# A gated linear-attention stage feeding a bilinear layer: larger bf16 product groups, paired state updates, a gate table in two parts

## The chip, the core and the metric

One NeuronCore of a Trainium2 chip. The metric is the device time of one execution in microseconds, the median over several runs; a profiled execution, taken apart from those runs, gives the span and all the rows below. TensorE is written PE, its weight loads PEld, VectorE DVE, ScalarE ACT, GpSimd POOL, and the queue of the sync engine, which issues all transfers here, SP.

## The reference

Inputs: q, k, v and an output gate of shape (4 batches, 8 heads, 768 steps, 40), two gates per step and head, and three weight matrices in float64 (two of 320x1536, one of 1536x320).

```python
for t in range(S):
    m_new = np.maximum(f_gate[:, :, t] + m, i_gate[:, :, t])
    f_stab = np.exp(f_gate[:, :, t] + m - m_new)
    i_stab = np.exp(i_gate[:, :, t] - m_new)
    m = m_new
    C = f_stab[..., None, None] * C + i_stab[..., None, None] * np.einsum('bhd,bhe->bhde', vt, kt)
    n = f_stab[:, :, None] * n + i_stab[:, :, None] * kt
    h_tilde = np.einsum('bhde,bhe->bhd', C, qt)
    denom = np.maximum(np.abs(np.einsum('bhd,bhd->bh', n, qt)[:, :, None]), 1.0)
    y[:, :, t] = sigmoid(o_gate[:, :, t]) * h_tilde / denom
x = y.transpose(0, 2, 1, 3).reshape(3072, 320)
out = ((x @ w_a) * (x @ w_b)) @ w_out
```

## The kernel before

**Chunks.** The 768 steps are cut into 6 time chunks of 128 rows for each of 4 batches: 24 chunks, numbered n = 4c + b. Within a chunk the recurrence becomes products: `pS` (keys times queries), multiplied by a decay matrix `E` (tile `gbc`), then `pV` (that times the values), plus `pI` (queries times the state before the chunk). `pU` is the chunk's addition to the state `cst`; `pT` and `pE` are transposes and the decay matrix of early chunks; `pX` transposes the finished rows into `xh` and `xl`. Chunks 0 to 5 use plain float32 products (`begin_a`, `begin_b`, `begin_i`, `begin_c`); from chunk 6 on every float32 operand is split into three bf16 parts and a product becomes several bf16 ones (`stage_a`, `stage_b`, `stage_i`, `stage_c`). A bf16 `pS` has 8 products for half the heads, a `pI` 16, a `pV` 48.

**The layer.** The 24 chunks are gathered in nine blocks of 2 or 3 chunks (256 or 384 rows). For each of 12 slices of the hidden width, `up` does 2 x 8 products `pu` (fp32r, from `xh`, `xl` and weight parts), DVE multiplies the two results into `g`, `gh` and `gl` are split off, and `down` does 3 products `pd` per chunk. Products `pu` and `pd` of 384, 256 and 320 columns are most of PE's work.

**Weights.** They come as float64 in 32 stages (`fetch`, `raw`). Each is turned into two fp32r parts: `high` on ACT, `low` on DVE or ACT, `join` on DVE, `lead_part` a copy on either, `low_part` a subtraction on DVE (tiles `cw` and `w`). `weights()` does stages 5 to 31 while block 0 runs; the last one, stage 31, is needed by the last `down` of block 0.

**Gates.** `first_gates` makes what chunks 0 to 3 need for their decay matrix. `later_gates` runs scans over steps 128 to 767 (32 rows of 640 on DVE, tiles `qks`), writes a table to DRAM (`g_dram`, read back by `load_g` as `gbc`), and transposes it (`ptg`) into `gtab`, which holds columns for weights of values (`w_col`), for decay (`a_col`), and so on. In `rest()` it runs before anything of chunk 2.

**The order.** Nothing is issued as written. A recorder (`Plan.add`) turns each call into a node; PE calls that follow each other and write the same tile (or carry `plan.pair`) form one node of at most 8. `Plan.run` is a list scheduler with a cost table, ranks and queues per engine; `settle` runs it 40 times with disturbed ranks and keeps the order with the least planned end; `emit` writes that order down. Operations of `copier` may go to ACT or DVE, those of `adder` to DVE or POOL. Where PE would idle early on, the plan inserts filler products into a tile `warm`. All instructions issued by `emit` carry line 522 (fillers 515), so the profile is read by tiles.

**State.** `stage_u` (line 1066) works chunk by chunk: 8 float32 products `pU` into half a bank, ACT copies or DVE updates `cst[b]`, and from chunk 2 on the state is split into bf16 parts (`cb`, `cr`), written to DRAM (`put_state`, `c_dram`) and read back (`get_state`, `cx`). `load(n + 2)` in `aside` fetches q, k and v two chunks ahead into three rotating tiles (`qk`, `va`).

Of the kernel before, what the change touches and what calls it, by code (L numbers as in the profile page):

```python
# [21 lines left out]
TURNS = 40  # L22
TRIALS = 4
# [7 lines left out]
SPELL = 3.4133  # L31

# [75 lines left out]
class Node:  # L108
    __slots__ = ("i", "eng", "alts", "calls", "by", "prev", "next", "table", "acc", "wide", "use", "pair", "least")

    def __init__(self, i, alts):
        self.i, self.alts, self.eng = i, alts, alts[0]
        self.calls, self.prev, self.next, self.acc = [], {}, [], []
        self.by = {e: [0.0, 0.0, 0.0, False] for e in alts}
        self.table, self.wide, self.use = None, True, 0.0


class Plan:
# [9 lines left out]
    def __init__(self, nc):  # L128
        self.nc, self.nodes, self.filler, self.bank = nc, [], None, None
        self.pair, self.least = False, 0.0  # L130
# [8 lines left out]
    def add(self, engines, op, args, kw):  # L139
# [13 lines left out]
        if not (  # L153
            alts[0] == "PE" and node is not None and node.eng == "PE" and len(node.calls) < 8
# [26 lines left out]
    def cost(self, node, by, eng, op, out, refs, args, kw):  # L181
# [5 lines left out]
        if eng == "PE":  # L187
            if op == "transpose":
                occ = 0.109
            else:  # L190
# [3 lines left out]
                elif "float32r" in f32[0]:  # L194
                    occ = cols / 2400 + 0.0135
# [7 lines left out]
            by[1] = 0.17  # L203
            plain = size[1] == 4 and op == "matmul" and "float32r" not in f32[0]
# [34 lines left out]
    def link(self):  # L239
        last, rings = {}, {}  # L240
        for node in self.nodes:
            for key, box, write in node.acc:
# [16 lines left out]
                mine.append((node, box, write))  # L259
        for ring in rings.values():  # L260
# [23 lines left out]
    def run(self, rank, forward=True, fixed=None, odds=None):  # L284
# [18 lines left out]
        order, count, filling = [], 0, False  # L303
# [21 lines left out]
        def choose(e, t):  # L325
# [6 lines left out]
            while ready[e] and found is None:  # L332
# [16 lines left out]
                else:  # L349
                    found = i  # L350
            for z in back:
                heapq.heappush(ready[e], z)
# [5 lines left out]
        while count < len(nodes):  # L358
# [56 lines left out]
            if e == "PE" and forward:  # L415
# [5 lines left out]
                z = free[e] + 0.2  # L421
                while filling and fixed is None:
                    w = int((z + phase) / SPELL)
                    z += 0.107 if used.get(w - 1, 0.0) >= 0.375 * SPELL * 2400 else 0.214
                    if z > t:
                        break
                    used[w] = used.get(w, 0.0) + 256
                    order.append(None)
                w = int((t + phase) / SPELL)
# [45 lines left out]
    def settle(self):  # L475
# [6 lines left out]
            (rng.uniform(0.98, 1.07, n), 1.0 + 0.025 * j, 0.1 * j, SPELL * j / TRIALS)  # L482
# [70 lines left out]
def kernel(  # L553
# [64 lines left out]
    cst = [wpool.tile([P, HH, DV], F32, name=f"cst{b}") for b in range(B)]  # L618
# [85 lines left out]
    def squash(c, b, nb):  # L704
        x = osig[c][:, b:b + nb, 0:DM]
        nc.scalar.activation(x, x, AF.Sigmoid)

# [43 lines left out]

    def later_gates():
# [8 lines left out]
        nc.scalar.copy(G[:, 0], gb3[0][:, 0])  # L761
        nc.scalar.copy(tab[BH:2 * BH, 0], gb3[0][:, 1])
        for c in range(1, NC):
# [6 lines left out]
        nc.sync.dma_start(g_dram.rearrange("c g t -> g c t"), G)  # L770
# [10 lines left out]
            tab[2 * BH:], tab[BH:2 * BH], G[:, :, P - 1:P].broadcast_to([BH, NC, P]), op=ALU.add  # L781
        )
        yield
        for half in range(2):
            pt = ps_dn.tile([P, 512], F32, tag="pd2", name="ptg")
            n3 = NC // 2
            for c in range(n3):
                nc.tensor.transpose(
                    pt[:, c * 3 * BH:(c + 1) * 3 * BH], tab[:, half * n3 + c, :],
                    ident[0:3 * BH, 0:3 * BH],  # L790
                )
            n0, n1 = (BH, n3 * 3 * BH) if half == 0 else (0, (n3 * 3 - 1) * BH)
# [4 lines left out]
        x = gtab[:, BH:].rearrange("p (c g) -> p c g", g=3 * BH)[:, :, 0:2 * BH]  # L797
# [9 lines left out]
    def g_col(c, b, x):  # L807
        return gtab[:, (3 * c + x) * BH + b * H:][:, 0:H]
# [7 lines left out]
    def a_col(c, b):  # L816
        return g_col(c - 1, b, 2)
# [165 lines left out]
    def stage_v(n):  # L983
        s = st[n]
        x = nat(n)[1]
        vr = apool.tile([P, H, DV], F32, tag="vr", name=f"vr{n}")
        vl = apool.tile([P, H, DV], BF16, tag="vl", name=f"vl{n}")
# [49 lines left out]
    def stage_c(n):  # L1037
# [4 lines left out]
        if c < NC - 1:  # L1042
            vw = apool.tile([P, H, DV], F32, tag="vw", name=f"vw{n}", bufs=1)
# [22 lines left out]
    def stage_u(n):  # L1066
        c, b = chunks[n]
        if c == NC - 1:
            return
        s = st[n]  # L1070
# [4 lines left out]
        pu = pU[:, 0:HH * DV].rearrange("p (h d) -> p h d", h=HH)  # L1075
        for h in range(H):
            r, _, x = half(h)
            nc.tensor.matmul(
                pu[r:r + 64, x], nat(n)[0][:, 1, h, :], s["vw"][:, h], start=True, stop=True
            )  # L1080
        t = cst[b]
        if c == 0:
            nc.scalar.copy(t, pu)
        else:
            nc.vector.tensor_tensor(
                t, t, dec[:, c - 1, b * HH:(b + 1) * HH].unsqueeze(2).broadcast_to([P, HH, DV]),
# [4 lines left out]
        if n + B < NF32:  # L1091
            return
        cb = apool.tile([P, 3, HH, DV], BF16, tag="cb", name=f"cb{n}", bufs=1)
        cr = apool.tile([P, H * DV], F32, tag="tmp", name=f"cr{n}")[:, 0:HH * DV]
        cr = cr.rearrange("t (h d) -> t h d", h=HH)
        nc.scalar.copy(cb[:, 2], t)
        nc.gpsimd.tensor_tensor(cr, t, cb[:, 2], op=ALU.subtract)
        yield
        if n < 8:
            nc.scalar.copy(cb[:, 1], cr)  # L1100
        else:
            nc.vector.tensor_copy(cb[:, 1], cr)
        nc.gpsimd.tensor_tensor(cb[:, 0], cr, cb[:, 1], op=ALU.subtract)
        states[n] = cb
        yield
# [46 lines left out]
    def stage_d(n):  # L1152
        s = st[n] if n < NS else st.pop(n)
# [25 lines left out]
    def aside(o, n):  # L1179
        if o == "L" and n + 2 < NCH and n + 2 > NS + 1:  # L1180
            load(n + 2)
        if o == "P":
            put_state(n - 1)
        if o == "G" and NE < n + 2 < NCH:
            load_g(n + 2)
        if o == "C":
            get_state(n - 1)
# [40 lines left out]
    def attention():  # L1228
        for n in range(NS, NCH):
# [369 lines left out]
```

## Time and profile before

| | before |
|---|---|
| median of 3 runs | 534.64 us (534.57 to 535.79) |
| profiled execution: own time | 534.12 us |
| profiled execution: span | 532.3 us |
| PE busy | 523.2 us (98%) |
| DVE busy | 411.4 us (77%) |
| ACT busy | 236.3 us (44%) |
| POOL busy | 147.9 us (28%) |

In a timeline row the first number is the start in microseconds from the span's beginning, the second the length, then engine, line, operation, tiles (output, arrow, inputs), shapes, and x with the number of instructions merged; a bracket tells idle time ahead and what ended it. PE's matmuls are pipelined: their records overlap, so what one costs is read from start to start, not from its length. A plain float32 product appears as two records.

### The profile page before, as it was taken

What the parts mean: (1) busy time and instruction counts of PE and PEld (TensorE: products, weight loads), DVE (VectorE), ACT (ScalarE), POOL (GpSimd) and SP (SyncE); (2) the same over time, 40 slices, a digit from 0 to 9 for tenths busy, and PEclk for the clock granted to TensorE, in tenths of its full rate; (3) what the DMA queues carried; (4) which work ended last, traced back from release to release, by engine and by line L of the source; (5) the groups of instructions that cost most, each with busy time, mean ns of one, the idle gap of its engine ahead of it and who ended that gap; (6) DMA issues with size and microseconds to landing.
All of it is one profiled execution on the core that took longest, in us unless ns stands there. A gap on an engine that the chain in (4) does not pass through costs nothing.

```text
span 532.3 us, 12505 instructions
## 1 busy us (share of the span) xinstructions
PE 523.2 (98%) x4862; PEld 497.1 (93%) x4862; DVE 411.4 (77%) x919; ACT 236.3 (44%) x568; POOL 147.9 (28%) x194
## 2 busy tenths in 40 slices
PE   8889999999999999999999999999999999999997
PEld 6679999999999999999999999999999999999997
DVE  5999999799979859888599776888489848843332
ACT  5759997543456142346243344543215515212111
POOL 2015134414326505534223423526050301000000
PEclk9899999999999999999999999999999999999999
DMA  9998866978696864886755766765537427000001
GB/s 172 305 245 182 238 167 135 137 148 165 117 188 129 148 146 104 155 158 104 169 105 97 158 119 157 155 99 114 130 73 140 93 41 156 2 1 25 2 1 37
DMA packets 198679, 66.77 MB, mean 125 GB/s; under 512 B 184252, under 2 KB 191900, under 8 KB 198620
## 3 DMA queue, kind: packets, MB, share of 16 engines
q1 hardware_dynamic: 198620, 65.98, 59.6%
q8 instruction: 38, 0.62, 0.5%
q14 instruction: 21, 0.17, 0.1%
HBM read 41.11 MB, written 5.97 MB: 88 GB/s over the span
## 4 chain that ended last, share of the span: by engine, by line
PE 81%; DVE 7%; issue 3%; DMA 2%; ACT 2%; SPq 1%; POOL 0%; ACTq 0%; DVEq 0%; POOLq 0%
PE pu L522 46%; PE pd L522 22%; PE pV L522 4%; PE pS L522 3%; PE pU L522 2%; DVE qks L522 2%; DVE w L522 2%; PE pI L522 2%; SPq L522 1%; PE pX L522 1%; DMA qk<-in_k_dram 1%; DVE cw L522 1%; DMA gbc<-g_dram 1%; DMA c_dram<-cb 1%; DVE osig L522 1%
## 5 line engine op out<-in xcount | busy, mean ns | idle before, releaser
L522 PE MATMUL pu<-xh,w 128*128 128x384 f32 (+1 forms) x1080 | 277.2, 325 | 0.1
L522 PE MATMUL pu<-xl,w 128*128 128x384 f32 (+1 forms) x648 | 203.9, 323 | 0.9 <-DVE xl L522 0.9
L522 PEld LDWEIGHTS pu<-xh,w 128*128 128x128 f32 x1080 | 190.0, 189 | 1.7 <-ACT xh L522 0.6
L522 PE MATMUL pd<-w,gh 128*128 128x320 f32 x576 | 135.1, 315 | 0.3 <-ACT gh L522 0.2
L522 PEld LDWEIGHTS pu<-xl,w 128*128 128x128 f32 x648 | 121.1, 189 | 1.4 <-DVE xl L522 1.2
L522 PEld LDWEIGHTS pd<-w,gh 128*128 128x128 f32 x576 | 97.0, 188 | 1.0 <-ACT gh L522 0.7
L522 DVE TENSOR_TENSOR g<-pu,g 128x384 f32<-128x384 f32 (+1 forms) x108 | 54.6, 506 | 53.4 <-PE pu L522 50.2
L522 ACT COPY g<-pu 128x384 f32<-128x384 f32 (+1 forms) x99 | 43.7, 442 | 113.8 <-PE pu L522 112.6
L522 PE MATMUL pd<-w,gl 128*128 128x320 f32 x288 | 86.6, 310 | 0.1
L522 ACT ACTIVATE gbc<-gbc,gtab 128x128 f32<-128x128 f32 x160 | 52.7, 394 | 3.3 <-POOL gbc L522 3.3
L522 PEld LDWEIGHTS pd<-w,gl 128*128 128x128 f32 x288 | 53.4, 188 | 0.3 <-DVE gl L522 0.3
L522 POOL TENSOR_TENSOR gl<-g,gh 128x384 fp32r<-128x384 f32 (+1 forms) x24 | 26.4, 1102 | 81.4 <-ACT gh L522 46.0
L522 DVE TENSOR_TENSOR gl<-g,gh 128x384 fp32r<-128x384 f32 (+1 forms) x84 | 46.4, 553 | 2.1 <-DVE gh L522 0.5
L522 ACT CAST gh<-g 128x384 fp32r<-128x384 f32 (+1 forms) x44 | 20.5, 465 | 39.9 <-DVE g L522 39.8
L522 DVE TENSOR_TENSOR gbc<-pS,gbc 128x512 f32<-128x512 f32 x48 | 32.6, 681 | 4.7 <-ACT gbc L522 3.7
L522 POOL TENSOR_TENSOR vr<-va 128x336 f32<-128x336 f32 x18 | 14.0, 775 | 79.0 <-PE pV L522 71.1
L522 PE MATMUL pV<-va,gbc 128*128 128x42 bf16 (+1 forms) x240 | 34.5, 221 | 0.0
L522 POOL TENSOR_TENSOR vw<-va,gtab 128x336 f32<-128x336 f32 x20 | 16.2, 808 | 64.9 <-PE pU L522 58.1
L522 PEld LDWEIGHTS <-T 120*128 120x128 bf16 x576 | 25.4, 97 | 7.6 <-issue 5.1
L522 DVE TENSOR_TENSOR gbc<-gbc,pb 128x512 f32<-128x512 f32 x36 | 29.4, 817 | 0.4 <-ACT pb L522 0.3
L522 DVE TENSOR_TENSOR pb<-gbc 128x512 bf16<-128x512 f32 x36 | 29.0, 806 | 0.3
L522 POOL TENSOR_SCALAR_AFFINE_SELECT gbc<-gbc 128x1024 f32<-128x1024 f32 x20 | 25.0, 1248 | 11.7 <-DMA gbc<-g_dram 11.7
(109 smaller groups left out, 768.7 us busy)
## 6 DMA issues: line engine op xcount, KB each, us to landing
gbc<-g_dram SPq DMA_DIRECT2D x20, 512.0 KB
qk<-in_q_dram SPq DMA_DIRECT2D x24, 160.0 KB
qk<-in_k_dram SPq DMA_DIRECT2D x24, 160.0 KB
va<-in_v_dram SPq DMA_DIRECT2D x24, 160.0 KB
osig<-in_o_gate_dram SPq DMA_DIRECT2D x24, 160.0 KB
raw<-in_moe_w_out_dram SPq DMA_DIRECT2D x12, 320.0 KB
out_dram<-o SPq DMA_DIRECT2D x24, 160.0 KB
raw<-in_moe_w_a_dram SPq DMA_DIRECT2D x8, 384.0 KB
```

The costliest lines, as they stand in the source:

```text
L522: f(*[real(x) for x in args], **{k: real(x) for k, x in kw.items()})
```

## The change

The planner gets other rules and the recorder larger groups; the state update takes two chunks at a time; the gate table for time chunk 0 is made apart from the rest.

- **Groups.** A PE node may hold 24 calls if its operand is bf16, 16 if paired, else 8 as before. In the scheduler a PE node whose first weight load is longer than the product ahead of it can hide is put back if another ready node, within `BAND` of its rank, is of the short kind; so short products follow each other. The cost table prices that load and the switch between full and half array. Filler rules are new (`GAP`, `FULL`, `LEAST`, `FORCED`), the disturbances in `settle` are other ones, and it makes 100 turns.
- **Pairs.** `stage_u` does nothing for even n; for odd n it issues the 16 products of chunks n-1 and n into one bank and does the update, the split and the writes for both at once (`cst2`). The key tile of chunk n-1 is therefore held longer: for odd n the load of k for chunk n+2 is issued at the end of `stage_u`, not by `aside`. `vw` gets two buffers, `vr` and `vl` one.
- **Gates.** `first_weights` makes the column that chunks 0 to 3 need (`pw`) from what `first_gates` left. `later_gates` now covers time chunks 1 to 5 alone and is called in `attention`, after chunk 2.

```diff
-TURNS = 40
+TURNS = 100
...
-            alts[0] == "PE" and node is not None and node.eng == "PE" and len(node.calls) < 8
+            alts[0] == "PE" and node is not None and node.eng == "PE" and len(node.calls) < (24 if getattr(refs[1], "size", 4) == 2 else 16 if self.pair else 8)
...
+            if e == "PE" and found is not None and tail < 0.06 and nodes[found].head > tail + 0.04:
+                like = [
+                    (k, i) for k, i in ready[e]
+                    if not done[i] and k < rank[found] + BAND and nodes[i].head < tail + 0.04
+                ]
+                if like:
+                    back.append((rank[found], found))
+                    found = min(like)[1]
...
+    def first_weights():
+        w0 = gf[:, 0:P]
+        nc.vector.tensor_scalar(w0, gb3[0][:, 1], gb3[0][:, 0, P - 1:], None, op0=ALU.add)
+        pw = ps_up.tile([P, NTB], F32, tag="pu", name="pw")[:, 0:BH]
+        nc.tensor.transpose(pw, w0, ident[0:BH, 0:BH])
+        nc.scalar.activation(gtab[:, BH:2 * BH], pw, AF.Exp)
...
-            nc.vector.tensor_copy(
-                gtab[:, half * (n3 * 3 - 1) * BH:][:, 0:n1 - n0], pt[:, n0:n1]
-            )
+            nc.copier.copy(gtab[:, (3 * cs[0] - 1) * BH:][:, 0:n1], pt[:, 0:n1])
...
     def stage_u(n):
         c, b = chunks[n]
-        if c == NC - 1:
+        if c == NC - 1 or n % 2 == 0:
             return
...
+        plan.pair = True
+        for j, m in enumerate((n - 1, n)):
+            for h in range(H):
+                r, _, x = half(h)
+                nc.tensor.matmul(
+                    pu[r:r + 64, j * HH + x], nat(m)[0][:, 1, h, :], st[m]["vw"][:, h],
+                    start=True, stop=True,
+                )
+        plan.pair = False
...
+        if n > NS and n + 2 < NCH:
+            load_qk(n + 2, (1,))
...
         if o == "L" and n + 2 < NCH and n + 2 > NS + 1:
-            load(n + 2)
+            whole = n % 2 == 0 or chunks[n][0] == NC - 1
+            load_qk(n + 2, (0, 1) if whole else (0,))
+            load_v(n + 2)
...
     def attention():
         for n in range(NS, NCH):
+            if n == NS + 1:
+                yield from later_gates()
+                load_g(NE)
...
     def rest():
-        gates = later_gates()
-        for _ in range(2):
-            next(gates)
-            yield
         yield from begin_a(NS)
         yield from begin_e(NS)
-        yield from gates
```

How the order moves, at three places. First DVE ahead of the first layer block; `xl0` is the low part of block 0's input, `qks2` and `qks3` hold the gates, `w` and `cw` are weights. Before, from the end of chunk 1 on:

```order
L522 TENSOR_TENSOR osig0_234<-pV1_346,osig0_234 128x320
L522 SCALAR_TENSOR_TENSOR qks2_88<-qks2_88 32x640
L522 SCALAR_TENSOR_TENSOR cw_390<-qks1_87,cw_390 128x384
L522 TENSOR_TENSOR qks2_88<-qks2_88 32x640
L522 TENSOR_TENSOR w4_359<-cw_338,w4_359 64x384
L522 TENSOR_TENSOR qks2_88<-qks2_88 32x640 x2
L522 SCALAR_TENSOR_TENSOR qks3_89<-one_102,qks2_88 32x128 x5
L522 TENSOR_TENSOR w1_387<-cw_363,w1_387 128x384
L522 TENSOR_TENSOR qks3_89<-qks2_88,qks3_89 32x640
L522 TENSOR_TENSOR xl0_398<-pX1_414,xh0_392 128x3x128
```

And of the change, from the same operation on:

```order
L559 TENSOR_TENSOR osig0_252<-pV1_356,osig0_252 128x320
L559 TENSOR_TENSOR w4_375<-cw_332,w4_375 64x384
L559 SCALAR_TENSOR_TENSOR cw_415<-qks1_87,cw_415 128x384
L559 TENSOR_TENSOR xl0_443<-pX0_411,xh0_421 128x3x128
L559 TENSOR_TENSOR w4_375<-cw_332,w4_375 64x384
L559 TENSOR_TENSOR w1_431<-cw_406,w1_431 128x384
L559 TENSOR_TENSOR xl0_443<-pX1_437,xh0_421 128x3x128
```

The ten gate operations on 32 rows stand between the last rows of chunk 1 and the second `xl0` before, and none does now; the first of them comes 17 rows behind it, within the weights and the first `g`. (The scans are listed as SCALAR_TENSOR_TENSOR here.)

Second, PE in block 2, where `pV8` is chunk 8's value product and `pd2`, `pu2` are the layer's. Before:

```order
L522 MATMUL pV8_2569<-vl8_2210,pb8_0_2407 128x42
L522 LDWEIGHTS gbc8_2070
L522 MATMUL pV8_2569<-va2_85,gbc8_2070 128x42
L522 MATMUL pd2_0_2438<-w7_580,gl2_2_2487 128x320
L522 LDWEIGHTS gbc8_2070
L522 MATMUL pV8_2569<-vr8_2196,gbc8_2070 128x42
```

With the change, the end of the same product:

```order
L559 MATMUL pV8_2505<-vr8_2261,gbc8_1973 128x42
L559 LDWEIGHTS pb8_1_2440
L559 MATMUL pV8_2505<-va2_85,pb8_1_2440 128x42
L559 LDWEIGHTS T9_1_2371
L559 MATMUL pS9_0_2562<-T9_0_2388,T9_1_2371 128x128
```

Before, a layer product stands inside `pV8`; now its 48 products stand in one piece, and `pS9` of the next chunk follows without a layer product between. Over the whole program the stretches of attention products between layer products were 150 and are 93; behind the first use of weight stage 31 they were 127 and are 72.

Third, PE's state products. Before, chunk 8's stand alone in the layer's products:

```order
L522 MATMUL pd2_2_2441<-w7_580,gl2_2_2487 128x320
L522 MATMUL pU8_2645<-vw8_2269,qk2_82 64x42 x8
L522 MATMUL pu2_5_0_2629<-xl2_1729,w10_697 128x384
```

With the change:

```order
L559 MATMUL pU9_2836<-vw8_2225,qk2_82 64x42 x8
L559 MATMUL pU9_2836<-vw9_2559,qk0_80 64x42 x8
```

Chunks 8 and 9 now follow each other; there were 20 such groups, and there are 10. Of the filler products of 256 columns there were 52, 28 of them in a row between the first three `pu` of block 0 and the fourth; there are 21, all ahead of the first `pu`.

More of the change, by code (lines that the diff above doesn't have):

```diff
@@ L108 @@
 class Node:
-    __slots__ = ("i", "eng", "alts", "calls", "by", "prev", "next", "table", "acc", "wide", "use", "pair", "least")
+    __slots__ = ("i", "eng", "alts", "calls", "by", "prev", "next", "table", "acc", "wide", "use", "pair", "least", "head", "tail", "mode")
     def __init__(self, i, alts):
@@ L203, in cost @@
             by[1] = 0.17
+            node.mode = 1 if refs[1].shape[0] <= 64 else 2 if out.shape[0] <= 64 else 0
+            node.tail = occ
+            if node.head is None:
+                node.head = (0.03 if size[1] == 2 else 0.107) / (2 if node.mode == 2 else 1)
             plain = size[1] == 4 and op == "matmul" and "float32r" not in f32[0]
@@ L259, in link @@
                 mine.append((node, box, write))
+        for a, b in self.orders:
+            self.edge(a, b, order=True)
         for ring in rings.values():
@@ L302, in run @@
         other = {"DVE": "POOL", "POOL": "DVE"}
-        order, count, filling = [], 0, False
+        order, count, filling, mode, tail, recent = [], 0, False, 0, 1.0, []
         def put(x, r):
@@ L420, in run @@
                     filling = False
-                z = free[e] + 0.2
+                z, forced = free[e], 0
                 while filling and fixed is None:
                     w = int((z + phase) / SPELL)
-                    z += 0.107 if used.get(w - 1, 0.0) >= 0.375 * SPELL * 2400 else 0.214
-                    if z > t:
+                    span = 0.107 if used.get(w - 1, 0.0) >= 0.375 * SPELL * 2400 else 0.214
+                    lately = sum(u for at_, u in recent if at_ > z - SPELL)
+                    if z + span < t - GAP and lately < FULL * SPELL * 2400:
+                        pass
+                    elif z > 3.0 and lately < LEAST * SPELL * 2400 and forced < FORCED:
+                        forced += 1
+                    else:
                         break
+                    recent.append((z, 256))
                     used[w] = used.get(w, 0.0) + 256
+                    z += span
                     order.append(None)
+                t = max(t, z)
+                recent.append((t, x.use))
+                del recent[:-60]
+                t += max(0.0, x.head - tail)
+                if x.mode != mode:
+                    t += 0.085
+                    mode = x.mode
+                tail = x.tail
                 w = int((t + phase) / SPELL)
@@ L706, in squash @@
         nc.scalar.activation(x, x, AF.Sigmoid)
+        if c == 0 and b < NS:
+            plan.orders += [(e, plan.nodes[-1]) for e in exps]
     def load_o(c):
@@ L1074, in stage_u @@
             pU = ps_at.tile([P, 512], F32, tag="pat", name=f"pU{n}")
[L1075 to L1081, printed above, removed]
+        pu = pU[:, 0:H * DV].rearrange("p (h d) -> p h d", h=H)
+        plan.pair = True
[7 more added lines that the diff above has]
+        plan.pair = False
+        t = cst2[b // 2]
         if c == 0:
@@ L1480 @@
     run(E[1], 2)
+    first_weights()
     run(S_[1])
@@ L1536, in rest @@
             if n == 0:
-                load(NS + 1)
+                load_qk(NS + 1, (0,))
+                load_v(NS + 1)
+            else:
+                load_qk(NS + 1, (1,))
         squash(0, NS, B - NS)
-        load_g(NE)
         yield from attention()
```

88 lines of the change are left out of this document (48 added, 40 removed).

## The prediction

> **What bounds the kernel now.** I read the page's totals first, then the windows by stage, then the timelines of PE and DVE where the windows show a change. From the page and from the windows (length, busy time and count of each engine, granted clock, DMA share, GB/s):
>
> ```profile
> span 532.3 us, 12505 instructions
> PE 523.2 (98%) x4862; PEld 497.1 (93%) x4862; DVE 411.4 (77%) x919; ACT 236.3 (44%) x568; POOL 147.9 (28%) x194
> 20.00:30.00 10.00, 8.85 (x49) 6.38 (x48) 9.65 (x18) 5.53 (x14) 0.00 (x0) 0.66 1.00 263
> 60.00:70.00 10.00, 9.80 (x89) 9.08 (x89) 9.67 (x26) 9.81 (x27) 3.86 (x5) 1.00 0.83 203
> 70.00:80.00 10.00, 10.00 (x91) 9.50 (x89) 9.88 (x24) 9.72 (x25) 2.65 (x3) 1.00 0.54 116
> 90.00:100.00 10.00, 10.00 (x105) 9.38 (x104) 7.68 (x25) 6.76 (x13) 3.54 (x5) 1.00 1.05 192
> 200.00:300.00 100.00, 100.00 (x972) 95.63 (x972) 84.91 (x180) 40.90 (x102) 37.37 (x46) 1.00 0.67 130
> ```
>
> PE is full from end to end, but not for one reason. From 90 us on, PE alone is full and the others have room. Up to 90 us DVE is as full as PE, and ACT with it: there the weights are converted. And in the window from 20 to 30 us PE's records are full while its clock is down to 0.66 and weight loads fill only 6.38 us. PE's timeline there:
>
> ```profile
> 23.27 1.01 PE L522 MATMUL pu<-xh,w 128*128 128x256 f32 x3
> 24.09 5.24 PE L515 MATMUL warm<-idle 128*128 128x256 bf16 x28
> 29.16 0.60 PE L522 MATMUL pT<-ident,qk 128*128 128x128 f32 x4
> 30.69 0.39 PE L522 MATMUL pu<-xl,w 128*128 128x256 f32 x1 [0.93 <-DVE xl L522]
> ```
>
> From 24.09 to 30.69 PE does fillers and one transpose group: 6.6 us in which the layer waits for `xl`. What DVE does until then:
>
> ```profile
> 21.71 1.54 DVE L522 TENSOR_TENSOR_SCAN qks<-qks 32x640 f32<-32x640 f32 x1
> ...
> 23.95 0.81 DVE L522 TENSOR_TENSOR qks<-qks 32x640 f32<-32x640 f32 x1
> ...
> 25.38 1.66 DVE L522 TENSOR_TENSOR qks<-qks 32x640 f32<-32x640 f32 x2
> 27.08 1.67 DVE L522 TENSOR_TENSOR_SCAN qks<-one,qks 32x128 f32<-32x128 f32 x5
> 28.68 0.52 DVE L522 TENSOR_TENSOR w<-cw,w 128x384 fp32r<-128x384 f32 x1
> 29.23 0.81 DVE L522 TENSOR_TENSOR qks<-qks,qks 32x640 f32<-32x640 f32 x1
> 30.08 0.56 DVE L522 TENSOR_TENSOR xl<-pX,xh 128x384 fp32r<-128x384 f32 x1
> 30.67 0.95 DVE L522 TENSOR_TENSOR qks<-qks 32x768 f32<-32x768 f32 x1
> ```
>
> The gate work stands in DVE's queue ahead of `xl`. From 30.69 us PE does layer products without a gap over 1 us to the last one:
>
> ```profile
> 528.76 0.31 PE L522 MATMUL pd<-w,gl 128*128 128x320 f32 x1
> ```
>
> **The gates.** Ahead of `xl` the ten gate operations go: 1.54 + 0.81 + 1.66 + 1.67 + 0.81 = 6.5 us of DVE. A copy of 0.6 us goes to ACT; a cast and the small operation of `first_weights` come, together some 0.8 us. Net 6.2 us, so `xl` would be ready at about 24.4 us instead of 30.6, and block 0 could run dense 6.3 us earlier. The fillers that stood in that place are gone in the order, so PE really has its work there.
>
> But the gate work isn't gone; it comes after the first `g`, and there DVE is full. What counts is when the weights are done, since block 0's last products need stage 31. Its last DVE operation and the first product that uses it, from the two timelines:
>
> ```profile
> 85.24 0.47 DVE L522 TENSOR_TENSOR w<-cw,w 128x320 fp32r<-128x320 f32 x1
> 87.13 0.46 PE L522 MATMUL pd<-w,gh 128*128 128x320 f32 x2
> ```
>
> It is ready at 85.7 and used at 87.1. So this is a second limit, 1.4 us behind which PE runs now. I count what stands ahead of that operation on DVE, before and with the change, by kind, and price each by its distance from start to start:
>
> ```profile
> 32.60 0.42 DVE L522 COPY gtab<-ptg 128x256 f32<-128x256 f32 x1
> 32.93 0.48 DVE L522 SCALAR_TENSOR_TENSOR cw<-qks,cw 128x320 uint32<-128x320 uint32 x1
> ...
> 36.87 0.68 DVE L522 COPY T<-pT 128x512 f32<-128x512 f32 x1
> 37.47 0.54 DVE L522 SCALAR_TENSOR_TENSOR cw<-qks,cw 128x384 uint32<-128x384 uint32 x1
> ```
>
> Four copies of `T` fewer (they go to ACT) at 0.60: -2.4. Two copies of `gtab` fewer at 0.33: -0.7. The last gate addition is 640 instead of 768 wide, 0.81 for 0.95, and the new small operation costs some 0.2: together +0.1. Casts of weights go both ways, about 0. Two casts of `gh`, one `xl`, and two single state operations now stand behind it, -1.7 by what their like take (0.24 to 0.47 each), and one wider cast of a state comes, +0.5. Sum -4.2 us, to about 81.5. So of the 6.3 us at the start only some 4 can reach the end of block 0: DVE has to do nearly the same work in either order. For the lag of 1.4 us I take half away, 0.7, since PE would now wait for the weight rather than the weight for PE; the ends are 0 and 1.4. Use of stage 31 then moves from 87.1 to 82.2, by **-4.9 us**. Bounds: -1.9 less if ACT, which gets the copies, becomes the later one; up to the whole of PE's own head start if DVE's idle and stretched times shrink (both are rivals below).
>
> **The groups.** What one break in the layer's products costs, read from PE's timeline in block 2, from start to start:
>
> ```profile
> 155.53 0.18 PE L522 MATMUL pV<-va,gbc 128*128 128x42 bf16 x1
> 155.56 0.39 PE L522 MATMUL pd<-w,gl 128*128 128x320 f32 x1
> 155.79 0.19 PE L522 MATMUL pV<-vr,gbc 128*128 128x42 bf16 x1
> 155.83 0.21 PE L522 MATMUL pV<-va,pb 128*128 128x42 bf16 x2
> ...
> 157.17 0.31 PE L522 MATMUL pd<-w,gh 128*128 128x320 f32 x1
> 157.31 0.31 PE L522 MATMUL pd<-w,gl 128*128 128x320 f32 x1
> 157.46 0.34 PE L522 MATMUL pu<-xl,w 128*128 128x384 f32 x1
> 157.64 0.51 PE L522 MATMUL pu<-xh,w 128*128 128x384 f32 x2
> ...
> 158.13 0.30 PE L522 MATMUL pd<-w,gl 128*128 128x320 f32 x1
> 158.36 0.67 PE L522 MATMUL pU<-vw,qk 128*64 128x42 f32 x16
> 158.96 0.44 PE L522 MATMUL pu<-xl,w 128*128 128x384 f32 x1
> 159.24 0.52 PE L522 MATMUL pu<-xh,w 128*128 128x384 f32 x2
> ```
>
> A `pd` among its like takes 0.145 us (157.17 to 157.46, two of them); the one behind a `pV` takes 0.23: +0.085. The first `pV` behind it takes 0.04 where the next ones take 0.025 (48 of them, one after the other): +0.015. A break costs 0.10 us. A state group costs more: the `pd` ahead of it takes 0.23, +0.085, and the `pu` behind it 0.28 for 0.18, +0.10.
>
> Behind the first use of stage 31 the order has 127 such stretches before and 72 now: 55 x 0.10 = 5.5 us. Seven fewer of them hold state products (15 and 8); beyond the 0.10 each saves 0.085 and some drain at its end, I take 0.13: 0.9. Together -6.4. Ahead of stage 31 the count hardly moves (22 and 20). Against this, work that was done by then now comes later: one chunk's value products in float32, four transposes and eight state products. The first is the largest:
>
> ```profile
> 15.52 2.02 PE L522 MATMUL pV<-va,gbc 128*128 128x42 f32 x16
> ```
>
> These 16 records take 1.85 us to the next start (17.37 us, fillers); four transposes some 0.45 at full clock, eight state products half of 0.6 or more: 2.2 to 2.9, taken as 2.7. From stage 31 to the end PE has thus 6.4 - 2.7 = **3.7 us** less to do. As PE alone is full there, this goes to the end in whole, if nothing else becomes late: DVE has about 15% of room from 200 to 300 us.
>
> **The state pairs elsewhere.** Each DVE operation on a state covers twice the columns at once; the fixed part saved is off the path. The split of two states is written in one go, so DMA issues stay as many. For odd n from 3 to 19, nine times, k's load goes out at the end of chunk n instead of its start; SP takes its queue in order, so what follows waits with it. The load's length, from the chain of waits:
>
> ```profile
> 97.52 4.38 DMA qk<-in_k_dram
> ```
>
> The key is needed when chunk n+2 is prepared, during chunk n+1. From 90 us to the end there are some 20 chunks in 440 us, 20 us each or more, so 4.4 us are covered; I cost it at nothing, and price the case in which they aren't, below. The single buffers of `vr` and `vl` I cost at nothing for the same reason (POOL, 37% busy, refills them).
>
> **The sum.** -4.9 - 3.7 = -8.6 us. Span 532.3 - 8.6 = 523.7; the profiled execution's own time, 534.12, becomes 525.5. The median of the runs shown, 534.64, lies 0.5 above that execution, so for the median I say **526.0 us**. Its own range, with the ends above: 521 to 529.
>
> **Rivals.**
> *PE alone decides from the start.* If DVE and ACT keep the weights ahead (the planner may have put the right ones first), block 0 runs dense from 24.4 us: -6.3, then -6.4 for groups, about -0.9 for a state group that now stands ahead of the first `pu`, and -2.6 for gaps of PE in the records between 30 and 87 us (an estimate from the distances between starts). Sum -16.2: 534.6 - 16.2 = 518.4. For it speaks that weight stages 1 and 3 to 9 stand 5 to 10 us earlier in DVE's sum; against it that stages 10 to 13 and 26 to 31 gain only 2 to 4, in windows where DVE is busy 9.67 to 9.88 of 10. Chance 0.18.
>
> *The gate work only moves.* ACT gets about 2 us more ahead of stage 31 and is as full as DVE from 60 to 80 us. If that eats the DVE gain, stage 31 comes no earlier and only the 3.7 us remain: 530.9. Chance 0.11.
>
> *The clock falls while PE waits for weights.* From 30.69 to 87.13 PE takes 56.4 us now; less 2.6 of gaps, 0.9 moved ahead and 2.7 moved behind, 50 us of work are left for the 57.8 from 24.4 to 82.2: 8 us of waiting, and no fillers. The window from 20 to 30 us, at 0.66, has 6.8 us at half clock, which costs 3.4 us of PE's pace. Three such stretches (10 us) would use up the 8 us of waiting and 2 more: 528. It decides only from the third on; chance 0.07. The Trainium skill, "TensorE: Matmul & The Clock Gate", section "HAM oscillation — how this bites in real kernels", says that an idle gap of more than about 3.4 us drops the array to half clock. By that rule a wait of 3.4 us or more for one weight would do it, and shorter ones would not; the trace of before shows the drop behind a stage of many short gaps instead.
>
> *The late key load decides: slower.* If each of the nine late loads makes PE wait, because SP's queue is held behind the state products and the transposes of the next chunk stand behind it, each costs up to the 4.4 us of the load. From 1 us each (8.6 / 9) the gain is gone; with 2 us each the sum is -8.6 + 18 = +9.4: 544. Against it: a chunk lasts some 20 us and the key is needed one chunk later. Chance 0.05.
>
> *It doesn't do what it says.* The order shows that stretches and gates did move, so this is left to the smaller gain above.
>
> **How the numbers follow.** The forecast has 0.59, the rivals 0.18, 0.11, 0.07 and 0.05. A difference of 0.3% (1.6 us) is about what a measurement of this kernel can tell from none. All cases but the late key load end over 1.6 us faster in their middle; of the smaller gain's 0.11 I leave 0.03 within 0.3%, and 0.02 of the key's 0.05 too. Faster 0.91, same 0.05, slower 0.04. For the range I take the forecast's own and most of the two cases beside it: 517.5 to 532.0.
>
> **What would show it.** Right: no filler behind the first `pu`; `xl` of block 0 at 24 to 25 us; PE waiting for `w` or late pieces in the windows from 30 to 80 us, DVE still over 9.5 of 10 there; stage 31 used at about 82 us; a `pd` of 0.23 us only at 72 places behind it. Wrong: PE without waits in these windows (then 518), stage 31 used at 86 us or later (then 531), a granted clock below 0.9 in a window after 30 us, or PE waiting for `T` or `pS` at chunks 5, 7, 9 and so on (the key loads).

## The result

| | before | with the change |
|---|---|---|
| median | 534.64 us (5 runs, 534.3 to 535.79) | 526.01 us (5 runs, 525.11 to 526.08) |
| profiled execution: own time, span | 534.12, 532.3 us | 526.01, 524.2 us |

The ratio is 0.9829, with an interval of 0.9815 to 0.9844: 8.6 us less, where 8.6 was forecast. The sum came out, but two of its terms did not: one was too large by 2.2 us, another too small by 1.7. By the spans the gain is 8.1 us; the other 0.5 us is that the execution profiled before lies 0.5 us under its median and the one after on it.

### The profile page after: what moved, and what is told of

Same layout as the page of the kernel before. It is cut to its first block, busy times and chain, and to the rows that moved or that the text cites. A ratio compares the mean times of both kernels' runs of the same rounds, so it can differ in the third digit from the quotient of the medians.

```text
span 524.2 us, 12355 instructions
## 1 busy us (share of the span) xinstructions
PE 512.2 (98%) x4831; PEld 494.8 (94%) x4831; DVE 411.5 (78%) x892; ACT 237.8 (45%) x563; POOL 136.8 (26%) x173
## 4 chain that ended last, share of the span: by engine, by line
PE 82%; DVE 9%; ACT 3%; DMA 3%; issue 2%; SPq 0%; DVEq 0%; ACTq 0%
PE pu L559 46%; PE pd L559 21%; PE pV L559 5%; PE pS L559 4%; DVE w L559 3%; DMA T<-qks 2%; PE pU L559 2%; PE pI L559 2%; DVE qks L559 1%; PE pX L559 1%; DVE cw L559 1%; DVE gbc L559 1%; DMA gbc<-g_dram 1%; DVE g L559 1%; PE warm L559 1%
## 5 line engine op out<-in xcount | busy, mean ns | idle before, releaser
L559 PE MATMUL pu<-xh,w 128*128 128x384 f32 (+1 forms) x1080 | 274.0, 324 | 3.7 <-DVE w L559 1.8
L559 PE MATMUL pd<-w,gh 128*128 128x320 f32 x576 | 132.0, 313 | 0.1
L559 PEld LDWEIGHTS pu<-xl,w 128*128 128x128 f32 x648 | 122.7, 190 | 0.1
L559 PE MATMUL pd<-w,gl 128*128 128x320 f32 x288 | 87.9, 311 | 0.2
L559 ACT COPY g<-pu 128x384 f32<-128x384 f32 (+1 forms) x95 | 41.9, 441 | 97.2 <-PE pu L559 94.6
L559 PEld LDWEIGHTS pd<-w,gl 128*128 128x128 f32 x288 | 53.9, 188 | 0.8 <-DVE gl L559 0.7
L559 DVE TENSOR_TENSOR gl<-g,gh 128x384 fp32r<-128x384 f32 (+1 forms) x87 | 50.4, 580 | 2.4 <-ACT gh L559 0.5
L559 ACT CAST pb<-gbc 128x512 bf16<-128x512 f32 x27 | 16.7, 619 | 56.6 <-DVE gbc L559 48.9
L559 POOL TENSOR_TENSOR gl<-g,gh 128x384 fp32r<-128x384 f32 (+1 forms) x21 | 21.1, 1003 | 54.2 <-DVE gh L559 26.5
L559 DVE TENSOR_TENSOR gbc<-gbc,pb 128x512 f32<-128x512 f32 x36 | 31.7, 881 | 1.0 <-ACT pb L559 0.8
```

The lines of the kernel that those rows point to most:

```text
L559: f(*[real(x) for x in args], **{k: real(x) for k, x in kw.items()})
```

## The profile after

The totals of the page:

```profile
span 524.2 us, 12355 instructions
PE 512.2 (98%) x4831; PEld 494.8 (94%) x4831; DVE 411.5 (78%) x892; ACT 237.8 (45%) x563; POOL 136.8 (26%) x173
```

PE's records hold 11.0 us less; DVE has as much work as before (411.4). The windows (PE, PEld, DVE, ACT, POOL, granted clock, DMA share, GB/s), first two of the kernel before, then those of the change:

```profile
40.00:50.00 10.00, 10.00 (x117) 9.57 (x113) 9.11 (x19) 9.62 (x24) 6.16 (x9) 1.00 0.80 171
50.00:60.00 10.00, 10.00 (x108) 9.51 (x107) 9.50 (x25) 9.97 (x23) 1.31 (x1) 1.00 1.03 288
```

```profile
20.00:30.00 10.00, 7.23 (x40) 6.29 (x39) 9.89 (x26) 9.76 (x23) 0.00 (x0) 0.66 1.06 277
...
40.00:50.00 10.00, 8.36 (x62) 7.33 (x61) 9.58 (x20) 8.63 (x18) 1.58 (x4) 1.00 1.06 312
50.00:60.00 10.00, 8.15 (x55) 7.61 (x56) 9.94 (x22) 8.64 (x20) 4.56 (x7) 0.83 1.01 274
...
70.00:80.00 10.00, 9.68 (x86) 8.70 (x85) 9.91 (x23) 9.49 (x28) 1.63 (x5) 1.00 0.51 76
...
200.00:300.00 100.00, 99.91 (x1011) 97.49 (x1010) 85.16 (x181) 40.43 (x97) 32.05 (x37) 1.00 0.69 136
```

From 20 to 30 and from 40 to 60 us PE now has holes where before it had fillers or products. DVE is fuller in all three windows. ACT is fuller from 20 to 30 us (9.76 for 5.53 of 10) and less full from 40 to 60 us. From 200 us on PE is still full, with 4% more products in the same 100 us (1011 records for 972). PE's timeline at the steps that the prediction named:

```profile
22.20 0.80 PE L559 MATMUL pX<-ident,osig 128*128 128x128 f32 x3 [1.03 <-DVE osig L559]
24.30 0.80 PE L559 MATMUL pu<-xh,w 128*128 128x256 f32 x2 [1.30 <-ACT xh L559]
24.90 1.50 PE L559 MATMUL pE<-cx 96*128 96x128 bf16 x12
26.16 0.56 PE L559 MATMUL pu<-xl,w 128*128 128x256 f32 x1
...
52.86 0.47 PE L559 MATMUL ptg<-ident,qks 96*128 96x96 f32 x3 [1.85 <-ACT gtab L559]
...
84.45 0.45 PE L559 MATMUL pd<-w,gh 128*128 128x320 f32 x2
...
520.67 0.31 PE L559 MATMUL pd<-w,gl 128*128 128x320 f32 x1
```

The 5.24 us of fillers are gone; the first low product starts at 26.16 instead of 30.69. The product at 84.45 is the first with weight stage 31 (87.13 before), the last one starts at 520.67 (528.76). So up to stage 31 the change takes 2.7 us, and from there to the end 436.2 us are needed instead of 441.6: 5.4 less. What DVE did for the first and the last of these:

```profile
24.86 0.55 DVE L559 TENSOR_TENSOR xl<-pX,xh 128x384 fp32r<-128x384 f32 x1
...
81.37 0.80 DVE L559 TENSOR_TENSOR w<-cw,w 128x320 fp32r<-128x320 f32 x1
```

`xl` is ready at 25.4 (30.6 before), stage 31 at 82.2 (85.7). PE's largest waits (total, times, longest):

```profile
PE ptg L559 <- ACT gtab L559: 1.9, 1, 1.9
PE pu L559 <- DVE w L559: 1.8, 2, 1.5
PE pu L559 <- ACT xh L559: 1.3, 1, 1.3
```

And what the larger groups look like, in block 2:

```profile
152.91 0.45 PE L559 MATMUL pd<-w,gh 128*128 128x320 f32 x2
153.20 0.19 PE L559 MATMUL pV<-va,pb 128*128 128x42 bf16 x1
153.24 0.18 PE L559 MATMUL pV<-vr,pb 128*128 128x42 bf16 x1
...
154.41 0.61 PE L559 MATMUL pS<-T,T 120*128 120x128 bf16 x8
154.83 0.39 PE L559 MATMUL pd<-w,gh 128*128 128x320 f32 x1
155.06 0.31 PE L559 MATMUL pd<-w,gl 128*128 128x320 f32 x1
155.21 0.30 PE L559 MATMUL pd<-w,gh 128*128 128x320 f32 x1
```

All 48 products of `pV` and the eight of `pS` stand in one piece, from 153.20 to 154.83. The `pd` behind them takes 0.23 us to the next start, the one after it 0.15: the price of a break is what it was, and it is paid once here.

## The experiments

Each run is a build of its own, and the planner makes a new order for each, so a part that is taken out also shuffles what is left. The medians are compared with runs of the kernel before on the same chip (534.8 to 535.4 us). "Ready" and "used" are the end of the last DVE operation on stage 31 (in e7 of the one on POOL) and the start of the first product with it; "rest" is from there to the last product; "breaks" are layer products behind another attention product than `pU`, in the rest, with what they take beyond the start-to-start time of their like (0.1745, 0.1195 and 0.1465 us for 384, 256 and 320 columns), summed over the trace.

| run | median us | ratio (interval) | ready | used | rest | breaks |
|---|---|---|---|---|---|---|
| before | 534.64 | | 85.7 | 87.1 | 441.6 | 116, 9.84 us |
| the change | 526.01 | 0.9829 (0.9815 to 0.9844) | 82.2 | 84.5 | 436.2 | 65, 5.53 us |
| e1_seed8 | 526.08 | 0.9833 (0.9793 to 0.9873) | 82.0 | 84.0 | 436.2 | |
| e2_no_groups | 537.18 | 1.0039 (1.0024 to 1.0053) | 86.9 | 87.8 | 443.6 | 115, 9.80 us |
| e3_no_pairs | 531.16 | 0.9921 (0.9899 to 0.9943) | 82.3 | 82.6 | 443.4 | 64, 5.44 us |
| e4_gates_early | 529.65 | 0.9892 (0.9869 to 0.9914) | 84.0 | 87.5 | 436.7 | |
| e5_planner_only | 535.23 | 0.9991 (0.9967 to 1.0015) | 89.1 | 91.2 | 439.3 | 63, 5.31 us |
| e6_old_planner | 530.55 | 0.9916 (0.9885 to 0.9948) | 82.0 | 85.1 | 439.9 | 98, 8.30 us |
| e7_pool_low | 528.27 | 0.9884 (0.984 to 0.9928) | 80.6 | 83.2 | 439.1 | |
| e8_light | 521.14 | 0.9729 (0.9704 to 0.9755) | 75.4 | 79.5 | 437.5 | |
| e9_fill_on | 527.38 | 0.985 (0.9825 to 0.9875) | 85.4 | 87.0 | 435.4 | |
| e10_one_bank | 525.80 | 0.9818 (0.9796 to 0.9841) | 83.4 | 83.4 | 437.6 | |
| e11_fill_one | 526.82 | 0.9839 (0.9817 to 0.9861) | 81.7 | 84.1 | 437.2 | |
| e12_light_fill | 522.67 | 0.9766 (0.9743 to 0.979) | 74.3 | 79.3 | 437.9 | |

The theory: groups shorten what follows stage 31, and the gates bring stage 31 forward as far as DVE's work on the weights allows. The rivals: the luck of one plan, the clock, the new waits in block 0, and the late key loads as a hidden loss.

**e1_seed8: another seed for the planner's disturbances.**

```diff
-        rng = np.random.default_rng(7)
+        rng = np.random.default_rng(8)
```

> The changed kernel with another seed of the planner's random ranks, nothing else; 88 stretches of attention products between layer products (93 with the change), 71 of them behind the first use of weight stage 31 (72). Theory (limits are DVE's weights up to stage 31, then PE): 526 us within 1.5, as the limits are the same. Rival (the gain is the luck of one plan): over 530 us. The difference to 526.0 is the noise of planning that the other runs are read against.

526.08 us (524.58 to 528.21), with the same rest. A second order gives the same time, so the result doesn't hang on the first one.

**e2_no_groups: groups as small as before, and no product put back for a like one.**

```diff
-BAND = 15.0
+BAND = -1e9
...
-  len(node.calls) < (24 if getattr(refs[1], "size", 4) == 2 else 16 if self.pair else 8)
+  len(node.calls) < 8
```

> The changed kernel with nodes of at most 8 calls again and the scheduler's preference for short products off; its prices, fillers, pairs and gates stay. 126 stretches behind stage 31 instead of 72. Theory (a break costs PE 0.10 us, state groups some more): 54 x 0.10 + about 0.5 = +5.9, 531.9 us. Rival (breaks are hidden, the gain is at the start): 526.

537.18 us: worse than either theory has it, and worse than the kernel before. The breaks are back in full, 4.3 us of the 11.2 lost. The rest has two large waits more (1.5 us near 117 us and 0.9 near 129), and block 0 loses 3.3. Its windows and its timeline show how:

```profile
40.00:50.00 10.00, 7.02 (x53) 6.30 (x52) 9.71 (x17) 6.66 (x14) 2.36 (x5) 0.95 1.04 235
50.00:60.00 10.00, 9.62 (x42) 8.95 (x41) 8.89 (x21) 9.18 (x21) 2.17 (x4) 0.50 0.62 133
60.00:70.00 10.00, 10.00 (x99) 9.15 (x97) 7.31 (x16) 6.01 (x17) 1.04 (x2) 0.87 1.00 260
```

```profile
47.89 0.39 PE L559 MATMUL ptg<-ident,qks 96*128 96x96 f32 x2 [2.61 <-DVE qks L559]
```

PE waits 2.6 us for the gates, which are now late work, and from 49.0 us runs at half clock for 13.7 us. New stages under new prices, but without groups, thus gain nothing in this order.

**e3_no_pairs: the state chunk by chunk again, k loaded with q and v.**

```diff
-        if c == NC - 1 or n % 2 == 0:
+        if c == NC - 1:
...
-            load_qk(n + 2, (0, 1) if whole else (0,))
-            load_v(n + 2)
+            load(n + 2)
```

> The changed kernel with the state update chunk by chunk as before, and k loaded with q and v again; groups and gates stay. 20 groups of state products instead of 10, 78 stretches behind stage 31 instead of 72. Theory: 6 x 0.10 and seven more state groups at 0.13 behind stage 31, +1.5: 527.5 us. Rival (the late key load makes PE wait): faster than the change, by up to 9 us.

531.16 us, 3.7 above the theory. Without the pairs and the late loads the kernel is 5.1 us slower, so the rival (without the late key loads it would be faster) falls. The rest is 7.2 us longer (block 0 1.9 shorter), but only 0.7 us of that is the price of single state groups at the layer products beside them (14 of them cost 1.47 us behind them, 7 pairs 0.76). Another 5.7 us is layer products that take longer to the next start for other reasons (6.04 us beyond their like in the rest, against 0.31). Late starts of over 0.1 us make only 1.1 of these 5.7 (3.3 us here, 2.2 in the change). The two largest here, and the window that has both:

```profile
185.37 0.55 PE L559 MATMUL pX<-ident,osig 128*128 128x128 f32 x3 [0.91 <-DVE gbc L559]
...
193.36 0.57 PE L559 MATMUL pd<-w,gh 128*128 128x320 f32 x2 [1.11 <-DVE gh L559]
```

```profile
180.00:200.00 20.00, 17.96 (x173) 16.71 (x172) 13.62 (x29) 6.93 (x20) 4.58 (x5) 1.00 0.58 118
```

DVE is busy for only 13.6 of 20 us there, so it is not short of room; why these two operations came late stays open. The other 4.6 us are no waits at all: from start to start, layer products take a little longer each, those of 384 columns 176.4 ns on average for 173.6 in the change (1077 and 1083 of them among their like), those of 256 and 320 columns 2.2 and 1.1 ns more. So most of what this run loses is not the work of the state products. Why the products take longer no run shows; the last section comes back to it.

**e4_gates_early: `later_gates` and `load_g` back where they stood.**

```diff
+        gates = later_gates()
+        for _ in range(2):
+            next(gates)
+            yield
         yield from begin_a(NS)
         yield from begin_e(NS)
+        yield from gates
```

> The changed kernel with the later gates' work put back ahead of chunk 2, as before; the first column apart, groups and pairs stay. Theory (the weights on DVE are the limit, the gate work has to be done before stage 31 in either order): stage 31 used 1 to 4 us later, 527 to 530 us. Rival (PE alone decides from the start, so the late start of block 0 counts in full): +6.3, 532.3 us.

529.65 us, as expected: 3.6 lost, and nearly all of it ahead of stage 31 (used at 87.5, rest 436.7). The way there is not the theory's alone: stage 31 is ready 1.8 us later than in the change but used 3.5 us behind that. PE's last large wait ahead of it (2.15 us, for `w`) ends at 31.4 us and PE is full from 40 to 60 us, so part of the loss is PE's own late start, as the rival has it, at about half its price.

**e5_planner_only: the kernel before under the new planner.** The classes of the recorder and planner and their constants are the change's, the stages are those of before.

> The kernel before with the changed planner (group sizes, preference for short products, prices, fillers, turns); gates early and states chunk by chunk as before. 77 stretches behind stage 31 instead of 127. Theory: 50 x 0.10 = -5.0 from the kernel before, 529.6 us, stage 31 used at about 87 us as before. Rival (the groups only pay with the other parts): 533 or more.

535.23 us (532.63 to 537.66 in ten runs; the profiled one took 536.05): no gain clear of that spread, a miss by 5.6. The groups do behind stage 31 what they should: 63 breaks for 116, 4.5 us less. But the rest is only 2.3 us shorter, as about half goes to pauses, and the start loses more than that. PE's timeline:

```profile
25.74 0.57 PE L559 MATMUL pX<-ident,osig 128*128 128x128 f32 x3 [3.70 <-DVE osig L559]
...
26.98 0.99 PE L559 MATMUL pu<-xh,w 128*128 128x256 f32 x3
27.77 2.95 PE L552 MATMUL warm<-idle 128*128 128x256 bf16 x16
30.91 0.39 PE L559 MATMUL pu<-xl,w 128*128 128x256 f32 x1 [0.20 <-DVE xl L559]
```

and DVE's:

```profile
22.22 1.54 DVE L559 TENSOR_TENSOR_SCAN qks<-qks 32x640 f32<-32x640 f32 x1
...
24.38 0.81 DVE L559 TENSOR_TENSOR qks<-qks 32x640 f32<-32x640 f32 x1
25.12 0.47 DVE L559 TENSOR_TENSOR osig<-pV,osig 128x320 f32<-128x320 f32 x1
...
30.30 0.56 DVE L559 TENSOR_TENSOR xl<-pX,xh 128x384 fp32r<-128x384 f32 x1
```

The gate scan now stands ahead of `osig`, which the transposes `pX` wait for, so the first `pu` comes at 27.0 instead of 23.3 and stage 31 is used 4.1 us later. My expectation took the start as fixed; with the gates ahead of block 0 it isn't, at least in this order.

**e6_old_planner: the stages of the change under the planner of before.**

> The changed kernel's stages (pairs, gate table in two parts, gates late) with the planner of before. 107 stretches behind stage 31, 14 with state products. Theory: 35 x 0.10 and a little for state groups over the change, 530 us. Rival (the start of block 0 is the gain): 526 to 527.

530.55 us, as expected. The stages alone give 4.3 us, and the planner on top of them 4.5: from 98 breaks to 65 it saves 2.8, and the rest is 3.7 shorter. On the stages of before the same planner gave nothing (e5). The parts don't add up one by one: in these orders the groups pay in full only once the gates are out of the start.

**e7_pool_low: the subtraction for the weights' low parts may go to POOL.**

```diff
-            nc.vector.tensor_tensor(
+            nc.adder.tensor_tensor(
                 w[other, jl], W[rows], w[rows, j].bitcast(F32), op=ALU.subtract
```

> The changed kernel; the subtraction that makes a weight's low part may go to POOL as well as DVE. Theory (DVE is the limit up to stage 31): stage 31 is ready 3 to 6 us earlier and the end comes with it until PE alone decides, 520 to 523 us. Rival (PE or ACT limits block 0): 526, and DVE below 9 of 10 between 30 and 80 us.

528.27 us, a miss. Stage 31 is ready 1.6 us earlier, not 3 to 6, and used 1.3 earlier, and the rest is 2.9 longer. PE's waits:

```profile
PE pu L559 <- DVE w L559: 2.7, 2, 1.5
PE pu L559 <- DVE g L559: 2.2, 2, 1.8
```

The relief for DVE came with an order that has more waits. This neither supports nor refutes the weights as a limit, so the next run takes the work away instead.

**e8_light: the conversion of stages 5 to 31 without its low part.**

```diff
                 high(x)
-                low(x)
-                join(x)
+                held[x][2] = step[x % len(step)][:, :held[x][1]]
                 yield x
```

> The changed kernel without the low bits of weight stages 5 to 31: low and join are left out, the parts are made from the first step alone, so these weights are other numbers; 13 us of DVE and some 15 of ACT go. Theory: no weight is late, block 0 runs at PE's own pace, the price of the prediction's first rival: 518 us within 2. Rival (PE was the limit all along): 526.

521.14 us, 4.9 below the change, all of it and a little more ahead of stage 31 (79.5 for 84.5), though 1.1 above the theory's range. Its windows, and PE's last wait in block 0:

```profile
40.00:50.00 10.00, 8.67 (x69) 8.47 (x68) 9.60 (x19) 6.72 (x15) 2.41 (x5) 1.00 1.03 212
50.00:60.00 10.00, 10.00 (x86) 9.33 (x86) 9.06 (x22) 7.17 (x18) 3.30 (x6) 1.00 0.97 238
```

```profile
49.78 0.50 PE L559 MATMUL pu<-xh,w 128*128 128x256 f32 x2 [1.33 <-ACT g L559]
```

ACT has room, no layer product waits for `w` any more (1.8 us in the change), and from 49.8 us PE works without a wait to stage 31. The work on the weights is a limit of block 0 in the change: shown by taking it away. The run takes work from DVE and ACT at once, so it doesn't tell which of the two it was. With this work gone, PE uses stage 31 4.1 us after it is ready: from 50 us on PE alone decides.

**e9_fill_on: the first state pair in another bank, so that fillers can run behind it.** In the change the pair `pU1` takes the fillers' bank, and PE's clock is at 0.66 from 20 to 30 us (half clock for 6.8 us from 23.2).

```diff
-            pU = ps_dn.tile([P, 512], F32, tag="pd2", name=f"pU{n}")
+            pU = ps_dn.tile([P, 512], F32, tag="pd0" if n < NS else "pd2", name=f"pU{n}")
```

> The changed kernel with the first pair's state products in another bank, so that the bank of the fillers stays free for them while PE waits for block 0's input (the profile after has the half clock from 23.2 to 30.0 us and waits of 1.0 and 1.3 us just ahead). Theory (up to stage 31 the weights on DVE limit, PE has waits to spare): the half clock at 23 us goes, stage 31 is ready at 82 us as before and its use comes to 82.5 to 84.5, so 524 to 526 us. Rival (PE and its clock limit block 0): the 6.8 us at half clock give back 3.4, 522.6 us.

527.38 us. The clock was not cured:

```profile
20.00:30.00 10.00, 6.14 (x37) 5.37 (x36) 9.87 (x23) 8.86 (x23) 0.00 (x0) 0.75 1.15 290
```

The half clock only starts later, at 25.0 us, again for 6.8 us, now within a wait of 3.8 us for `xh`. The run decides nothing.

**e10_one_bank: the five transposes `ptg` in one bank with one copy.** The 1.9 us wait in the change is for the copy that frees the bank between its two halves.

```diff
-        for half in range(2):
...
+        pt = ps_dn.tile([P, 512], F32, tag="pd2", name="ptg")
+        for c in range(1, NC):
+            nc.tensor.transpose(
+                pt[:, (c - 1) * 3 * BH:c * 3 * BH], tab[:, c, :], ident[0:3 * BH, 0:3 * BH]
+            )
+        n1 = (3 * (NC - 1) - 1) * BH
+        nc.copier.copy(gtab[:, 2 * BH:][:, 0:n1], pt[:, 0:n1])
```

> The changed kernel with the five transposes of the gate table in one bank and one copy, instead of two turns of one bank (the profile after has PE waiting 1.9 us for the copy between them, at 50.7 us). Theory (weights limit): the wait goes, another takes its place before stage 31, 525 to 526.5 us. Rival (each wait of PE in block 0 counts in full): 524.1 us.

525.80 us, as expected. The wait is gone, and the one for a weight near 43 us is 2.1 us instead of 1.5: the same time as the change.

**e11_fill_one: e9 and e10 together.**

> Both edits at once: first pair in another bank, gate transposes in one bank. Theory (weights limit): stage 31 ready at 80 to 82 us and used at once, 523.5 to 525 us. Rival (PE and its clock limit block 0): 3.4 + 1.9 less, 520.7 us.

526.82 us, above both forecasts. This is the clearest test of the clock and of that wait, because here both are gone:

```profile
20.00:30.00 10.00, 8.00 (x93) 6.70 (x92) 9.76 (x24) 9.52 (x23) 0.00 (x0) 1.00 1.00 270
...
40.00:50.00 10.00, 8.96 (x75) 8.49 (x73) 9.73 (x21) 9.51 (x21) 1.69 (x4) 1.00 1.04 289
50.00:60.00 10.00, 9.15 (x70) 7.83 (x69) 9.78 (x21) 8.86 (x21) 3.28 (x6) 1.00 0.94 221
```

The clock is full in every window, and stage 31 is used at 84.1 (84.5). In this order neither is the limit: what they give back goes into a first `pu` 1.4 us later (25.7 us) and into other waits of PE (1.0 us for a key, 0.7 for `gbc`, 0.6 for `g`, 1.0 for `w`). The last of them is for a weight, and it ends at 75.6 us. The theory missed too: stage 31 is used 2.4 us after it is ready, not at once.

**e12_light_fill: e8, e9 and e10 together.**

> Both edits on the kernel whose weight stages 5 to 31 leave out their low bits (other numbers, 13 us of DVE and 15 us of ACT less). Theory: with the weights out of the way PE's clock and waits are what is left in block 0, so here the edits count: 521.1 less 3 to 4, 517 to 518 us, near the 518.4 of the prediction's first rival. Rival (something else on DVE or ACT limits block 0): 520 to 521.5 us, with the half clock gone and waits in its place.

522.67 us: 1.5 above e8 and above both forecasts, and half clock is back in this plan, from within a wait of 3.3 us for `xh`.

```profile
20.00:30.00 10.00, 6.45 (x44) 5.64 (x42) 9.27 (x18) 8.93 (x19) 0.00 (x0) 0.76 0.98 270
...
50.00:60.00 10.00, 8.88 (x71) 8.59 (x71) 9.14 (x26) 7.74 (x18) 1.14 (x3) 1.00 1.09 225
```

```profile
51.20 0.39 PE L559 MATMUL pu<-xh,w 128*128 128x256 f32 x1 [1.12 <-DVE g L559]
```

Once the weights are light, the last wait of PE in block 0 ends here, at 51.2 us, and from there PE works without one to stage 31, which is ready 5 us before it is used. So behind 51 us PE alone decides, as in e8; ahead of it the waits for `xh` and `g` do. Of all the versions that compute the whole reference, none is measurably faster than the change (e10's interval and the change's overlap).

## Why the prediction was right, and where it wasn't

**The gates: right in kind, 1.0 us too large.** No filler stands behind the first `pu`; `xl` is ready at 25.4 instead of the forecast 24.4. What stands ahead of it came later: the first `pu` itself starts at 24.30, 1.0 later than before, behind waits for `osig` and `xh` (1.03 and 1.30 us in the rows above). `xh`, which `xl` needs, is ready on ACT at 24.25, and DVE has two weight subtractions in its queue ahead of `xl`, from 23.80 until it starts at 24.86.

**Stage 31: the term that was mis-sized.** Forecast were -4.2 for ready and -0.7 for the lag between ready and used, together -4.9. Measured are -3.5 and +0.9, together -2.7. DVE was done with stage 31 within 0.7 us of the forecast. What failed is the step "PE would now wait for the weight rather than the weight for PE", by which half of the lag should go. PE does wait for weights, but not for this one. Its last wait in block 0 is for stage 27, and behind it PE works for 7.2 us without a wait until it comes to stage 31:

```profile
77.25 0.51 PE L559 MATMUL pu<-xh,w 128*128 128x256 f32 x2 [0.31 <-DVE w L559]
```

So the end of block 0 hangs on earlier weights and waits (`ptg`, stage 12, `xh`) and on PE's own work behind them. The 8 us of waiting that the forecast has were there only in part: layer products of block 0 take 8.4 us beyond their like, 2.5 before, but 2.7 of the 8.4 are products that ran in the stretches at half clock. The two largest waits end at 43.0 and 52.9 us. That the work on weights holds block 0 is shown by e8 (-4.9 us without it) and, from the other side, by e11, where a full clock and one wait less bring nothing. The gates' place is worth 3.6 us by e4, partly through PE's start.

**The groups: the price held, the sum was too small by 1.7.** The price of a break, 0.085 us at the layer product behind it, is the same in every run: 9.84 us over 116, 5.53 over 65, 5.31 over 63. Split by starts in the trace, the rest went like this:

| from stage 31 on | forecast us | measured us |
|---|---|---|
| breaks | -5.5 | 116 to 65 of them: -4.3 |
| state products in pairs | -0.9 | beside them 2.32 to 0.85, eight of them 0.60 to 0.53: -2.5 |
| work that came to stand behind stage 31 | +2.7 | `pV` 1.71, `pT` 0.44, eight `pU` 0.53: +2.7 |
| other short products | 0 | -0.4 |
| layer products over 0.1 us late | 0 | 0 to 2.2: +2.2 |
| all other layer products | 0 | -3.1 |
| sum | -3.7 | -5.4 |

The work that moved cost what was forecast. The breaks gave 1.2 us less: the 0.015 us that I had added for the first short product of a group does not show in the sum of the short products, and 51 breaks went, not 55. The pairs gave 1.6 us more, since they save inside the group too. The last two terms I had at nothing, and they are the larger ones. "If nothing else becomes late" did not hold: 2.2 us do. That is more than made up by about 2250 layer products that take 1.4 ns less each on average from start to start, 173.6 for 175.5 ns at 384 columns. This I had no term for, and that it makes up for stage 31 is luck.

**Costed at nothing.** The late key loads: no wait of PE for a key or its transpose stands among the change's waits, and e3, which has no late loads, is slower. In e11 one transpose of chunk 3 waits 1.0 us for its key, until 45.8 us; no other run with the late loads has a wait put down to a key. POOL, which refills `vr` and `vl`, fell from 147.9 to 136.8 us, with no wait of PE for it.

**The rivals.** PE alone from the start (518.4): refuted, PE has holes from 40 to 60 us. The gate work only moves (530.9): refuted, stage 31 came 3.5 us earlier and e4 shows the place to matter. The clock: it did fall once more, 3.4 us from 53.9 us, the window at 0.83 above, a sign that I had set down against myself. It was to decide from the third stretch of 6.8 us on; there were one and a half, the first from 23.2 us now over layer products and no longer over fillers. They cost 2.7 us at these products, and e11 without them isn't faster.

**Slips of the working.** They change nothing in the sum. The net of the gates is 6.3 us by its own terms, not 6.2, and the chances by their own shares are 0.92 and 0.03, not 0.91 and 0.04. From 20 to 30 us PE's records fill 8.85 of 10 us, which is not all, and ACT is as full as PE only from 40 to 80 us (7.15 of 10 from 30 to 40, 6.89 from 80 to 90).

What the prediction didn't see is how much the parts need each other. It added gates and groups as if each brought its share alone. Alone, the planner brings nothing (e5) and the stages 4.3 (e6); together 8.6, each by one order.

## What to carry to other kernels

Price a break in a stream of large products by the extra start-to-start time of the product behind it, and count the breaks in the order: that product of two small numbers held in every run here. Compare the ordinary products of two builds as well, before you put a difference down to the part that you took out. A term that ends at a wait ("the weight comes earlier by so much") needs the other side too, since the engine that no longer waits there may arrive late from waits further ahead. Where a search makes the order, test a part both ways, taken out of the new kernel and put alone into the old one, and leave differences of 1 to 2 us in 526 unread: e1 alone spreads over 3.6 us, and e9 and e11, both meant to help, ended 1.4 and 0.8 us above the change.

## What was not expected of the hardware

Half clock came after shorter waits than one rule has it. In e2 the longest wait ahead of 13.7 us of half clock is 2.6 us; in the change 1.85 us, ahead of 3.4 us of it. The Trainium skill, "TensorE: Matmul & The Clock Gate", section "HAM oscillation — how this bites in real kernels", gives an idle gap of more than about 3.4 us as the condition. The two such gaps in these traces do lie beside half clock (3.7 us in e5, 3.8 in e9), but in e2 and in the change it came without one, in stretches where PE's records fill 7 to 8.4 of 10 us and the longest gap is the one named. And a full clock was worth nothing where the array had to wait anyway (e11: 1.00 in every window, 526.82 us).

Ordinary layer products don't take the same time in every build. Those of 384 columns, among their like and behind stage 31, take 175.5 ns from start to start in the kernel before and 174.9 in e5, 176.4 in e3, and 173.6 or 173.7 in the change and in each of the ten other runs. Before, 143 of 1027 take 180 ns or more; with the change 5 of 1083 do. The three groups of builds also place `xh` and `xl` at three different addresses in on-chip memory, but no run moves a tile alone, so the cause stays open.
